# A decode block on one core: queries projected once per head in a loop, engines' code moved to new blocks, one store

## The chip, the core and the metric

The kernel runs on one core of a Trainium2 chip. The metric is the device time of one execution in microseconds; the core's engines are TensorE (PE, with its weight loads as PEld), VectorE (DVE), ScalarE (ACT), GpSimd (POOL) and SyncE (SP), and 16 DMA engines move data between HBM and SBUF.

## The reference

One decode step for two sequences (B = 2): pre-LayerNorm attention over a long cache, then a SwiGLU feed-forward, both with a residual. All data is float32.

```python
h  = x + A(_layernorm(x))            # x: [2, 1, 512]
h2 = h + B(_layernorm(h))

# A: 32 heads of 128, cache of 8192 keys and values per head and sequence
q = (x @ wq).reshape(B, 1, 32, 128).transpose(0, 2, 1, 3)      # wq: [512, 4096]
scores = einsum("bhqd,bhkd->bhqk", q, k_cache) * 128 ** -0.5   # [2, 32, 8192, 128]
o = einsum("bhqk,bhkd->bhqd", softmax(scores), v_cache)
A = o.transpose(0, 2, 1, 3).reshape(B, 1, 4096) @ wo           # wo: [4096, 512]

# B: F = 1792
B = (silu(x @ w_gate) * (x @ w_up)) @ w_down
```

The two caches are 268 MB each, wq and wo 8.4 MB each, the three feed-forward weights 3.7 MB each.

## The kernel before, in words

The program is written engine by engine: `do(engine, fn, sem)` appends an instruction to that engine's list, `wait(engine, point)` a wait for a semaphore's value, and `emit` writes the lists out. Nothing reorders them. All large loads stand in one list, `loads`, which SP issues in order on one DMA queue at the end of the function (L578 to L581); ahead of a load SP waits for `freed[...]`, the point at which the last reader of the slot is done.

There are three large SBUF slots of 64 KB in each partition: `kslot[0]`, `kslot[1]` and `vslot`. The loads are: wq into `vslot`; K0 (in two halves) and K1 into the key slots; then, in turn, V0, K2, V1, K3 and so on, V always into `vslot`, K into the key slot that its number names; at the end the last V, wo, w_gate, w_up and w_down. V0 waits for `freed["wq", 0]`, the last matmul that reads wq. V(i) waits for the matmuls of V(i-1), K(i) for VectorE's last reading of K(i-2).

A unit of work (32 in all, `U`) is two heads of one sequence. Half of the partitions (`HALF[0]`) hold the keys of one head, the other half those of the next. VectorE multiplies the keys by the query (L419) and sums over the 128 columns (L428), each in two parts. TensorE and ScalarE make the softmax (`pe_scores`, `softmax`), and TensorE multiplies by the values (`pe_values`, L329: 32 matmuls in four column groups of PSUM). TensorE's 31 first units are a hardware loop (`Fori`, L348); the last unit and the tail (wo, gate, up, down) are written out.

Ahead of the units comes the query projection. VectorE's multiply needs each query in all 64 partitions of its half. So the kernel before broadcasts each of the eight columns of the normalized and transposed x over 64 columns (`xT`, `xb`, L273 to L278) and uses these as weights: for each group of four head pairs and each sequence, eight matmuls (four chunks of 512 inputs, two halves) write a query into 64 equal rows of each half of a PSUM bank (L292, 64 matmuls). ScalarE copies each bank to `qsb` (L303). `q_done` holds these eight points, and `freed["wq", 0]` the last matmul.

The result is stored by two DMAs, one for each sequence, from SP and from ScalarE (L588). wo comes in three loads (`WO`: 20, 8 and 4 blocks), each waited for by the matmul that first reads it (L478).

Of the kernel before, what the change touches and what calls it, by code (L numbers as in the profile page):

```python
# [13 lines left out]
class Program:  # L14
# [16 lines left out]
    def wait(self, engine, *points):  # L31
        for s, value in points:
            if self.known[engine].get(s, 0) < value:
                self.known[engine][s] = value
                self.steps[engine].append(lambda e, s=s, v=value: e.wait_ge(s, v))  # L35
# [17 lines left out]
def decode_block(nc, x, k_cache, v_cache, wq, wo, w_gate, w_up, w_down, out):  # L53
    B, _, D = x.shape
    _, H, S, DH = k_cache.shape
    F = w_gate.shape[1]
    assert DH == P and B == 2 and D == 512 and F == 14 * P and H == 32 and S == 64 * P
    DC = D // P
# [4 lines left out]
    HP = P // 2  # L63
    NJ = S // HP
    U = B * H // 2
    MQ = H // 2
    HALF = (slice(0, HP), slice(HP, P))

# [8 lines left out]
    def sbuf(name, *shape, align=32):  # L77
        return nc.alloc_sbuf_tensor(name, list(shape), F32, align_bytes=align).ap()
# [25 lines left out]
    scores = [sbuf(f"s{n}", P, NJ) for n in range(2)]  # L104
# [4 lines left out]
    r = sbuf("r", P, 1)  # L109
# [9 lines left out]
    wide = [psum(f"wide{n}", P, D) for n in range(2)]  # L119
    bank = [psum(f"bank{n}", P, D) for n in range(4)]  # L120
# [16 lines left out]
    def alone(name):  # L137
        return g.sem(name)
# [3 lines left out]
    landed = {}  # L142
    freed = {}
    loads = []

    def k_src(cache, i):
        m, b = divmod(i, B)
# [70 lines left out]
    wait("scalar", ident_done)  # L218
    do("scalar", lambda e: e.dma_start(xs, x.rearrange("b s d -> (b s) d")), x_in := alone("x"), 16)
    p0 = do("gpsimd", lambda e: e.memset(sides, 0.0), s_pool)  # L220
    do("vector", lambda e: e.memset(nscale, -SCALE))
    half_done = do("vector", lambda e: e.memset(mhalf, -0.5), s_dve)
    wait("vector", ident_done)
# [46 lines left out]


    wait("vector", p)
    p = do("vector", lambda e: e.tensor_copy(xT, yt), s_dve)  # L273
    wait("vector", p)
    xb = osb.rearrange("p (c m) -> p c m", c=DC * B)
    xb_done = do(
        "vector",
        lambda e: e.tensor_copy(xb, xT.rearrange("p c b -> p (c b)")[:, :, None].to_broadcast([P, DC * B, HP])),  # L278
        s_dve,
    )  # L280
    wait("tensor", xb_done, landed[("wq", 0), 0])
    wqv = vslot.rearrange("p (c m k d) -> p c k m d", c=DC, k=2, d=DH)
    q_done = []
    for n, (m, b) in enumerate((m, b) for m in range(0, MQ, 4) for b in range(B)):
        ps = wide[n % 2].rearrange("p (j d) -> p j d", d=DH)
        if n > 1:
            wait("tensor", q_done[n - 2])
        for c in range(DC):
            for k in range(2):
                p = do(  # L290
                    "tensor",
                    lambda e, ps=ps, c=c, k=k, m=m, b=b: e.matmul(  # L292
                        ps[HALF[k]],
                        xb[:, c * B + b, :],
                        wqv[:, c, k, m : m + 4, :],
                        start=(c == 0),
                        stop=(c == DC - 1),
                    ),
                    s_pe if c == DC - 1 and k == 1 else None,
                )  # L300
        wait("scalar", p)
        q_done.append(
            do("scalar", lambda e, ps=ps, m=m, b=b: e.activation(qsb[:, b, m : m + 4, :], ps, AF.Copy), s_act)  # L303
        )
    freed["wq", 0] = p
    wait("tensor", consts_done)


# [1 line left out]
    base = g.count[s_pe]  # L310
# [34 lines left out]

    def pe_rounds(e):
        e.sem_inc(s_v, -16)
        with nc.Fori(0, U - 1, engines=[PE], head_slot={PE: 0}):  # L348
            pe_scores(e)
            e.wait_ge(s_v, 16)  # L350
            pe_values(e, vslot)
            pe_outputs(e)
            e.sem_inc(s_dve_pe, -2)
            e.sem_inc(s_act_pe, -2)
            e.sem_inc(s_v, -16)
        pe_scores(e)
        e.wait_ge(landed[("v", U - 1), 0][0], 16)
        pe_values(e, v_last)
        pe_outputs(e)
# [50 lines left out]
    for i in range(U):  # L410
        m, b = divmod(i, B)
        parts = 2
        n = NJ // parts
        wait("vector", q_done[m // 4 * B + b])
        for c in range(parts):
            wait("vector", landed[("k", i), c if i == 0 else 0])
            kt = k_view(i, c * n, n)
            qb = qsb[:, b, m, :][:, None, :].to_broadcast([P, n, DH])
            mult = do("vector", lambda e, kt=kt, qb=qb: e.tensor_tensor(kt, kt, qb, op=OP.mult), s_dve)  # L419
# [51 lines left out]
    for c in range(H):  # L471
# [3 lines left out]
        t = c % 4  # L475
# [21 lines left out]
    wait("scalar", normed)  # L497
    h1_done = do("scalar", lambda e: e.activation(h1, attn, AF.Copy), s_act)
# [28 lines left out]
    for t in range(4):  # L527
        do(
            "tensor",
            lambda e, t=t: e.matmul(  # L530
                f_ps[32 * t : 32 * t + 32, :], ident[:B, :32], h1[:, t * P : (t + 1) * P], start=True, stop=False
            ),
        )
    sg = rest[:, D : D + FQ]
# [43 lines left out]
    for item, e_, dst, src, sem in loads:  # L578
        if item in after:
            wait("sync", freed[after[item]])  # L580
        do("sync", lambda e, dst=dst, src=src: e.dma_start(dst, src), sem, 16)  # L581
    stored = []
    for b, engine in enumerate(("sync", "scalar")):
        wait(engine, res_done)
        stored.append(
            do(
                engine,
                lambda e, b=b: e.dma_start(out[b, 0, :].rearrange("(t m) -> t m", t=4), res[b::32, :]),  # L588
                alone(f"out{b}"),
                16,  # L590
            )
        )

    wait("sync", *stored)
# [42 lines left out]
```

## Time and profile before

| | |
|---|---|
| median of 3 runs | 1309.95 us (1309.79 to 1310.46) |
| the profiled execution | 1309.7 us |
| its span, first to last instruction | 1308.4 us |
| busy: PE, DVE, ACT | 434.1, 1131.3, 80.4 us |
| moved by DMA | 564.79 MB, 432 GB/s over the span |

In the rows, L329 is line 329 of the program before. A row of the timeline gives start, duration, engine, line, operation, output and inputs, and in brackets the engine's idle time ahead of it and what ended it. A row of DMA issues ends with the us from issue to landing. A float32 matmul leaves two records, and as many weight loads.

### The profile page before, as it was taken

Reading aid. Unit: us, or ns where it says so; the run is one execution under the profiler, and the core shown is the slowest. Engines: PE = TensorE matmul, PEld = TensorE weight load, DVE = VectorE, ACT = ScalarE, POOL = GpSimd, SP = SyncE. Lnnn points to the kernel's source line nnn. Section 1 sums busy time; section 2 is a strip of 40 time slices with the busy share of each in tenths; the row PEclk is TensorE's granted clock in tenths of the full one; section 3 lists DMA queues with packets and bytes.
Section 4 is the critical chain, followed back from the end, with each engine's and each line's share of the span. In section 5 each row is a group of like instructions: output and inputs, shape, how many; then the busy total and the mean of one; then the engine's idle time right before and its main releaser. Section 6 shows DMA issues by size and latency. Waiting matters only on the chain.

```text
span 1308.4 us, 6704 instructions
## 1 busy us (share of the span) xinstructions
PE 434.1 (33%) x2952; PEld 135.6 (10%) x2952; DVE 1131.3 (86%) x246; ACT 80.4 (6%) x271; POOL 2.9 (0%) x13
## 2 busy tenths in 40 slices
PE   3633223333223333311333321233332233332276
PEld 1210001011001011100101100001100010110022
DVE  1999988889888889988888988888998888898841
ACT  0100000000000000000000000000000000000010
POOL 0000000000000000000000000000000000000000
PEclk9865566666556666656666656666655666665578
DMA  9999999999999999999999999999999999999998
GB/s 403 440 437 439 427 447 423 443 423 445 421 445 425 441 435 431 443 427 443 423 445 421 445 425 441 433 433 443 427 441 425 441 425 441 429 439 435 431 423 371
DMA packets 11118, 564.79 MB, mean 432 GB/s; under 512 B 1242, under 2 KB 1250, under 8 KB 1636
## 3 DMA queue, kind: packets, MB, share of 16 engines
q1 hardware_dynamic: 11096, 564.67, 99.7%
q8 instruction: 5, 0.08, 0.0%
q14 instruction: 5, 0.04, 0.0%
q10 hardware_dynamic: 12, 0.01, 0.0%
HBM read 564.66 MB, written 0.00 MB: 432 GB/s over the span
## 4 chain that ended last, share of the span: by engine, by line
DMA 53%; DVE 45%; PE 1%; SPq 0%; issue 0%; DVEq 0%
DMA kslot<-in_A_k_cache_dram 48%; DVE kslot L419 22%; DVE s L428 22%; DMA kslot<-in_A_v_cache_dram 3%; DMA kslot<-in_B_w_down_dram 3%; PE opart L329 1%; DVE gm L372 0%; SPq L581 0%; DVE r L398 0%; PE bank L564 0%; DVE m L436 0%; DVE kslot L575 0%; DVEq L35 0%
## 5 line engine op out<-in xcount | busy, mean ns | idle before, releaser
L419 DVE TENSOR_TENSOR kslot<-kslot,qsb 128x8192 f32<-128x8192 f32 x64 | 555.6, 8681 | 119.5 <-DMA kslot<-in_A_k_cache_dram 119.5
L428 DVE TENSOR_REDUCE s<-kslot 128x64 f32<-128x8192 f32 x64 | 555.2, 8675 | 0.1
L329 PE MATMUL opart<-vslot,pz 128*8 128x512 f32 x1984 | 285.3, 740 | 246.5 <-DMA vslot<-in_A_v_cache_dram 246.5
L321 PE MATMUL bank<-gm,nscale 1*64 1x1 f32 x64 | 11.8, 250 | 358.4 <-DVE gm L372 358.4
L329 PEld LDWEIGHTS opart<-vslot,pz 128*8 128x8 f32 x1984 | 55.3, 104 | 450.4 <-DMA vslot<-in_A_v_cache_dram 249.1
L319 PE MATMUL bank<-ident,m 128*1 128x128 f32 x64 | 18.7, 395 | 168.1 <-DVE m L436 168.1
L321 PEld LDWEIGHTS bank<-gm,nscale 1*64 1x64 f32 x64 | 9.1, 199 | 374.4 <-DVE gm L372 374.4
L341 PE MATMUL bank<-rdiag,osb 128*128 128x2 f32 x256 | 33.7, 254 | 26.3 <-ACT osb L405 26.3
L400 ACT ACTIVATE rdiag<-fold,r 128x8 f32<-128x8 f32 x32 | 9.6, 301 | 484.6 <-DVE r L398 484.6
L379 ACT ACTIVATE nb<-bank 128x1 f32<-128x1 f32 x32 | 5.5, 171 | 551.6 <-PE bank L322 551.6
L341 PEld LDWEIGHTS bank<-rdiag,osb 128*128 128x128 f32 x256 | 31.0, 191 | 56.0 <-ACT osb L405 56.0
L292 PE MATMUL wide<-vslot,osb 128*64 128x512 f32 x128 | 29.9, 630 | 9.4 <-DMA vslot<-in_A_wq_dram 9.4
L324 PE MATMUL bank<-rs,sides 128*128 128x1 f32 x64 | 18.8, 363 | 41.5 <-ACT pz L385 41.5
L385 ACT ACTIVATE pz<-s,nb 64x128 f32<-64x128 f32 x64 | 25.5, 399 | 1.4
L405 ACT ACTIVATE osb<-opart 128x512 f32<-128x512 f32 x32 | 19.1, 597 | 72.4 <-PE opart L329 72.4
L324 PEld LDWEIGHTS bank<-rs,sides 128*128 128x128 f32 x64 | 16.1, 313 | 44.2 <-ACT pz L385 44.2
L319 PEld LDWEIGHTS bank<-ident,m 128*1 128x1 f32 x64 | 2.7, 81 | 171.6 <-DVE m L436 171.6
L292 PEld LDWEIGHTS wide<-vslot,osb 128*64 128x64 f32 x128 | 10.5, 146 | 28.0 <-issue 28.0
L385 ACT ACTIVATION_READ_ACCUMULATOR pz<-s,nb 64x1 f32 x64 | 11.8, 184 | 0.0
L322 PE MATMUL bank<-gm,nscale 1*64 1x1 f32 x64 | 11.8, 250 | 0.0
L235 DVE BATCH_NORM_STATS2 ln_stats<-attn 2x6 f32<-2x512 f32 x1 | 0.7, 686 | 11.4 <-PE attn L491 11.4
L451 DVE TENSOR_TENSOR om<-oT,quarter 128x256 f32<-128x256 f32 x1 | 0.4, 426 | 11.4 <-ACT oT L407 11.4
(60 smaller groups left out, 104.3 us busy)
## 6 DMA issues: line engine op xcount, KB each, us to landing
kslot<-in_A_k_cache_dram SPq DMA_DIRECT2D x2, 4096.0 KB, 35.8
vslot<-in_A_wo_dram SPq DMA_DIRECT2D x1, 5120.0 KB, 22.0
kslot<-in_B_w_gate_dram SPq DMA_DIRECT2D x1, 3584.0 KB, 31.7
kslot<-in_B_w_up_dram SPq DMA_DIRECT2D x2, 1792.0 KB, 37.5
vslot<-in_A_wo_dram SPq DMA_DIRECT2D x1, 2048.0 KB, 26.4
kslot<-in_B_w_down_dram SPq DMA_DIRECT2D x2, 1024.0 KB, 29.9
vslot<-in_A_wo_dram SPq DMA_DIRECT2D x1, 1024.0 KB, 28.4
kslot<-in_B_w_down_dram SPq DMA_DIRECT2D x1, 768.0 KB, 32.3
```

Of the source, the lines that this page charges most:

```text
L292: lambda e, ps=ps, c=c, k=k, m=m, b=b: e.matmul(ps[HALF[k]], xb[:, c * B + b, :], wqv[:, c, k, m : m + 4, :], start=(c == 0), stop=(c == D ...
L319: e.matmul(mrow, m1, ident, start=True, stop=True).then_inc(s_pe, 1)
L321: e.matmul(nb_ps[HALF[0]], nscale, gm[:, 0:1], start=True, stop=True)
L322: e.matmul(nb_ps[HALF[1]], nscale, gm[:, 1:2], start=True, stop=True).then_inc(s_pe, 1)
L324: e.matmul(den, sides.rearrange("p w a -> p (w a)"), rs, start=True, stop=True).then_inc(s_pe, 1)
L329: inst = e.matmul(opart[32 * t : 32 * t + 2 * W, :], pz[:, w, :], t_v[:, w * W * DH : (w + 1) * W * DH], start=(w < 4), stop=(w >= NW - 4),)
L341: inst = e.matmul(ot_ps, osb[:, a * DH : (a + 1) * DH], rdiag[:, a::W], start=(a == 0), stop=(a == W - 1))
L385: lambda e, k=k, h=h: e.activation(pz[h, :, k * W : (k + 1) * W], s[h].rearrange("p (w a) -> p w a", a=W), AF.Exp, bias=nb[h], scale=SCALE ...
L400: do("scalar", lambda e: e.activation(rdiag, diag, AF.Copy, scale=r))
L405: do("scalar", lambda e: e.activation(osb, opart, AF.Copy), s_act_pe)
L419: mult = do("vector", lambda e, kt=kt, qb=qb: e.tensor_tensor(kt, kt, qb, op=OP.mult), s_dve)
L428: lambda e, kt=kt, s=scores[i % 2][:, c * n : (c + 1) * n]: e.tensor_reduce(s, kt, axis=AX.X, op=OP.add),
```

## The change

**Queries.** The transposed x goes into `xq`, zero but for one column for each sequence and half, so that a matmul's weights are [128, 4]: eight matmuls (four chunks, two halves) leave the queries of four head pairs in four PSUM rows (half, sequence) of `wide[0]`. ScalarE copies these rows to `qrow`. Two more matmuls, one for each sequence, with a 0/1 matrix `pick` [4, 128] as weights, spread each query over the 64 rows of its half, into `q_ps`, and ScalarE copies both to `qsb`. This body runs four times (`NG`) in a hardware loop on TensorE. A semaphore `q` brings ScalarE's copies back to the loop. `freed["wq", 0]` is the eighth matmul of the last trip. VectorE's first unit waits for the first copy, all others for the last (`q_done` has two points).

**Code.** `next_block` puts the first instructions of TensorE, VectorE and ScalarE (there behind the load of x) at the start of the next block of instructions, by a branch over the padding. The loop of the units on TensorE begins at slot 80 of its block, before at slot 0.

**The rest.** x is loaded ahead of everything on ScalarE, without a wait for the identity matrix. GpSimd prepares `xq`, `pick` and `place`. The tail puts the two sequences at rows 0 and 16 of each group of 32 (`LANE`), before at 0 and 1, so that one DMA can store both. wo comes in two loads of 20 and 12 blocks.

```diff
+    LANE = 32 // B
+    place = sbuf("place", B, 32)
+    xq = sbuf("xq", P, DC, 2, 2 * B)
-    xT = sbuf("xT", P, DC, B)
+    qrow = osb[: 2 * B, :]
+    pick = om[: 2 * B].rearrange("p b (k r) n -> p b k (r n)", k=2)
+    s_q = g.sem("q")
...
+    BLOCK = {"tensor": 256, "vector": 128, "scalar": 128}
+    def next_block(engine):
+        do(engine, lambda e: e.addr_align(BLOCK[engine], offset=0, max_nops=0))
+    next_block("tensor")
+    next_block("vector")
...
-    WO = ((0, 20), (20, 8), (28, 4))
+    WO = ((0, 20), (20, 12))
...
+    do("scalar", lambda e: e.dma_start(xs, x.rearrange("b s d -> (b s) d")), x_in := alone("x"), 16)
+    next_block("scalar")
...
-    wait("scalar", ident_done)
-    do("scalar", lambda e: e.dma_start(xs, x.rearrange("b s d -> (b s) d")), x_in := alone("x"), 16)
+    xq_zero = do("gpsimd", lambda e: e.memset(xq, 0.0), s_pool)
...
-    wait("tensor", xb_done, landed[("wq", 0), 0])
+    lanes = xq.rearrange("p c k (l b) -> p c (k l) b", b=B)[:, :, ::3, :]
+    wait("vector", p, xq_zero)
+    xq_done = do("vector",
+        lambda e: e.tensor_copy(lanes, yt[:, :, None, :].to_broadcast([P, DC, 2, B])), s_dve)
+    wait("tensor", xq_done, pick_done, landed[("wq", 0), 0])
     wqv = vslot.rearrange("p (c m k d) -> p c k m d", c=DC, k=2, d=DH)
+    QM = 4
+    NG = MQ // QM
+    q_ps = [wide[1], bank[1]]
+    q_base = g.count[s_pe]
+    def pe_queries(e):
+        e.sem_inc(s_q, B)
+        with nc.Fori(0, NG, engines=[PE]) as n:
+            for j, (c, k) in enumerate((c, k) for c in range(DC) for k in range(2)):
+                inst = e.matmul(
+                    wide[0][: 2 * B, :].rearrange("p (j d) -> p j d", d=DH),
+                    xq[:, c, k, :],
+                    wqv[:, c, k, bass.ds(n * QM, QM), :],
+                    start=(j == 0), stop=(j == 2 * DC - 1))
+            inst.then_inc(s_pe, 1)
+            e.wait_ge(s_q, B + 1)
+            for b in range(B):
+                inst = e.matmul(q_ps[b], pick[:, b].rearrange("p k r -> p (k r)"), qrow,
+                                start=True, stop=True)
+            inst.then_inc(s_pe, 1)
+            e.sem_inc(s_q, -(B + 1))
-    for n, (m, b) in enumerate((m, b) for m in range(0, MQ, 4) for b in range(B)):
-        ps = wide[n % 2].rearrange("p (j d) -> p j d", d=DH)
-        if n > 1:
-            wait("tensor", q_done[n - 2])
...
+    for n in range(NG):
+        wait("scalar", (s_pe, q_base + 2 * n + 1))
+        do("scalar", lambda e: e.activation(qrow, wide[0][: 2 * B, :], AF.Copy), s_q)
+        wait("scalar", (s_pe, q_base + 2 * n + 2))
+        for b in range(B):
...
+    freed["wq", 0] = (s_pe, q_base + 2 * NG - 1)
...
-        with nc.Fori(0, U - 1, engines=[PE], head_slot={PE: 0}):
+        with nc.Fori(0, U - 1, engines=[PE], head_slot={PE: 80}):
...
-        wait("vector", q_done[m // 4 * B + b])
+        wait("vector", q_done[min(i, 1)])
...
-    hT_done = do("vector", lambda e: e.tensor_copy(hT[:, :, :B], yt), s_dve)
+    hT_done = do("vector", lambda e: e.tensor_copy(hT[:, :, ::LANE], yt), s_dve)
...
-    for b, engine in enumerate(("sync", "scalar")):
-        wait(engine, res_done)
...
+    wait("sync", res_done)
+    rows = out.rearrange("b s (t m) -> t (b s) m", t=4)
+    stored = do("sync", lambda e: e.dma_start(rows, res[::LANE, :]), alone("out"), 16)
+    wait("sync", stored)
```

TensorE's rows of the projection before: each names its line, output, inputs and what it waits for; `wide` is the PSUM bank, `vslot` holds wq, `osb` the broadcast x, and act is ScalarE's semaphore.

```order
L253 MATMUL bank<-ident,ln_y 128x2 x3
L292 MATMUL wide<-vslot,osb 64x512 [waits v,dve]
L292 MATMUL wide<-vslot,osb 64x512 x15
L292 MATMUL wide<-vslot,osb 64x512 [waits act]
L292 MATMUL wide<-vslot,osb 64x512 x7
...
L348 ISA [waits pool]
L348 UNCONDITIONAL_BRANCH
```

After, the same place holds the loop's body once (here `osb` is `qrow`, `om` is `pick`, ISA a step on registers, and q the semaphore of ScalarE's copies; two of the eight query matmuls are shown):

```order
L332 UNCONDITIONAL_BRANCH [waits v,dve,pool]
L332 ISA
L334 MATMUL wide<-vslot,xq 4x512
L334 ISA
L334 MATMUL wide<-vslot,xq 4x512
...
L344 MATMUL wide<-osb,om 128x512 [waits q]
L344 MATMUL bank<-osb,om 128x512
L332 REGISTER_ALU
L332 COMPARE_AND_BRANCH
```

The half-width matmuls (64 rows of output) are gone, the wait for ScalarE moved from every second group's start into the middle of each trip, and the wait for wq (v) stands ahead of the loop. ScalarE's rows at the same place, before:

```order
L303 ACT_TABLE_LOAD
L303 ACTIVATE qsb<-wide 128x512 [waits pe] x8
L379 ACTIVATE nb<-bank 128x1 [waits pe]
L385 ACTIVATE pz,rs<-s,nb 64x32x4 [waits pool,act]
L385 ACTIVATE pz,rs<-s,nb 64x32x4
```

and after:

```order
L354 ACT_TABLE_LOAD
L354 ACTIVATE osb<-wide 4x512 [waits pe]
L360 ACTIVATE qsb<-wide 128x512 [waits pe]
L360 ACTIVATE qsb<-bank 128x512 [waits act]
L354 ACTIVATE osb<-wide 4x512 [waits pe]
L360 ACTIVATE qsb<-wide 128x512 [waits pe]
L360 ACTIVATE qsb<-bank 128x512
```

Eight copies became twelve, three for each trip: the four rows, then one bank for each sequence.

More of the change, by code (lines that the diff above doesn't have):

```diff
@@ L217, in decode_block @@
     )
-    wait("scalar", ident_done)
-    do("scalar", lambda e: e.dma_start(xs, x.rearrange("b s d -> (b s) d")), x_in := alone("x"), 16)
+    xq_zero = do("gpsimd", lambda e: e.memset(xq, 0.0), s_pool)
+    p0 = do("gpsimd", lambda e: e.memset(pick, 0.0), s_pool)
+    wait("gpsimd", p0)
+    pick_done = do(
+        "gpsimd",
+        lambda e: e.affine_select(
+            out=pick,
+            in_=pick,
+            compare_op=OP.not_equal,
+            fill=1.0,
+            base=0,
+            pattern=[[-1, B], [-B, 2], [0, HP]],
+            channel_multiplier=1,
+        ),
+        s_pool,
+    )
     p0 = do("gpsimd", lambda e: e.memset(sides, 0.0), s_pool)
+    p1 = do("gpsimd", lambda e: e.memset(place, 0.0), s_pool)
     do("vector", lambda e: e.memset(nscale, -SCALE))
@@ L268, in decode_block @@
         p0 = do("gpsimd", lambda e, t=t, value=value: e.memset(t, value), s_pool)
-    consts_done = p0
[L272 to L276, printed above, removed]
+    wait("gpsimd", p1)
+    p0 = do(
+        "gpsimd",
+        lambda e: e.affine_select(
+            out=place,
+            in_=place,
+            compare_op=OP.not_equal,
+            fill=1.0,
+            base=0,
+            pattern=[[-1, 32]],
+            channel_multiplier=LANE,
+        ),
+        s_pool,
+    )
@@ L282, in decode_block @@
     wqv = vslot.rearrange("p (c m k d) -> p c k m d", c=DC, k=2, d=DH)
-    q_done = []
-    for n, (m, b) in enumerate((m, b) for m in range(0, MQ, 4) for b in range(B)):
-        ps = wide[n % 2].rearrange("p (j d) -> p j d", d=DH)
-        if n > 1:
-            wait("tensor", q_done[n - 2])
[L288 to L304, printed above, removed]
@@ L305, in decode_block @@
-    freed["wq", 0] = p
+    QM = 4
[10 more added lines that the diff above has]
+                    wqv[:, c, k, bass.ds(n * QM, QM), :],
+                    start=(j == 0),
+                    stop=(j == 2 * DC - 1),
+                )
+            inst.then_inc(s_pe, 1)
+            e.wait_ge(s_q, B + 1)
+            for b in range(B):
+                inst = e.matmul(
+                    q_ps[b], pick[:, b].rearrange("p k r -> p (k r)"), qrow, start=True, stop=True
+                )
+            inst.then_inc(s_pe, 1)
+            e.sem_inc(s_q, -(B + 1))
@@ new lines, in decode_block @@
+    g.steps["tensor"].append(pe_queries)
+    q_done = []
+    for n in range(NG):
[3 more added lines that the diff above has]
+        for b in range(B):
+            told = (n, b) in ((0, 0), (NG - 1, B - 1))
+            c = do(
+                "scalar",
+                lambda e, n=n, b=b: e.activation(
+                    qsb[:, b, n * QM : (n + 1) * QM, :], q_ps[b].rearrange("p (j d) -> p j d", d=DH), AF.Copy
+                ),
+                s_act if told else s_q,
+            )
+            if told:
+                wait("scalar", c)
+                do("scalar", lambda e: e.sem_inc(s_q, 1))
+                q_done.append(c)
@@ L306, in decode_block @@
+    freed["wq", 0] = (s_pe, q_base + 2 * NG - 1)
+    g.count[s_pe] = q_base + 2 * NG
     wait("tensor", consts_done)
@@ L530, in decode_block @@
             lambda e, t=t: e.matmul(
-                f_ps[32 * t : 32 * t + 32, :], ident[:B, :32], h1[:, t * P : (t + 1) * P], start=True, stop=False
+                f_ps[32 * t : 32 * t + 32, :], place, h1[:, t * P : (t + 1) * P], start=True, stop=False
             ),
@@ L581, in decode_block @@
         do("sync", lambda e, dst=dst, src=src: e.dma_start(dst, src), sem, 16)
-    stored = []
-    for b, engine in enumerate(("sync", "scalar")):
-        wait(engine, res_done)
[L585 to L594, printed above, removed]
+    wait("sync", res_done)
+    rows = out.rearrange("b s (t m) -> t (b s) m", t=4)
+    stored = do("sync", lambda e: e.dma_start(rows, res[::LANE, :]), alone("out"), 16)
+    wait("sync", stored)
     ids = sorted(s.num for s in g.sems)
```

3 lines of the change are left out of this document (2 added, 1 removed).

## The prediction

> **What bounds the kernel now.** I read the DMA part of the page first, then the chain, the timeline of the first 130 us, the DMA view by stretches, and the timeline of the tail. The page, then the chain:
>
> ```profile
> q1 hardware_dynamic: 11096, 564.67, 99.7%
> DMA 53%; DVE 45%; PE 1%; SPq 0%; issue 0%; DVEq 0%
> ```
>
> Queue q1, which carries every large load, is busy for 99.7% of the span on all 16 DMA engines. The chain calls 45% DVE because it follows K0 to K2 through VectorE, but VectorE then waits for keys again. So the time is: when the stream starts, 564.67 MB at its steady rate, stretches in which the queue is empty or an engine of it lags, and what comes after the last byte. No saving on a compute engine counts unless it moves one of these. The timeline, by start, duration and engine:
>
> ```profile
> 0.73 0.40 SPq L581 DMA_DIRECT2D vslot<-in_A_wq_dram  x1
> 22.80 29.86 PE L292 MATMUL wide<-vslot,osb 128*64 128x512 f32 x128 [9.44 <-DMA vslot<-in_A_wq_dram]
> 32.44 8.69 DVE L419 TENSOR_TENSOR kslot<-kslot,qsb 128x8192 f32<-128x8192 f32 x1 [18.42 <-DMA kslot<-in_A_k_cache_dram]
> 52.69 0.33 SPq L581 DMA_DIRECT2D vslot<-in_A_v_cache_dram  x1
> 67.21 0.33 SPq L581 DMA_DIRECT2D kslot<-in_A_k_cache_dram  x1
> 82.09 8.59 PE L329 MATMUL opart<-vslot,pz 128*8 128x512 f32 x64 [3.49 <-DMA vslot<-in_A_v_cache_dram]
> 120.70 9.76 PE L329 MATMUL opart<-vslot,pz 128*8 128x512 f32 x64 [7.08 <-DMA vslot<-in_A_v_cache_dram]
> ...
> vslot<-in_A_wq_dram SPq DMA_DIRECT2D x1, 21.9
> ```
>
> V0 and V1 are used as they land, 38.61 us apart with one K load between: 19.3 us for 8.39 MB. wq landed at about 22.7, and K0, K1 and V0 are three such loads, so V0 was due at 80.6. It came at 82.1: the last of its engines lost about 1.45 us on the way. The DMA view of three stretches (0 to 100, 100 to 1250, 1250 to the end) shows what else ran:
>
> ```profile
> q8 instruction: 2, 0.03, 0.1%
> ...
> q14 instruction: 4, 0.03, 0.0%
> ...
> q8 instruction: 3, 0.05, 0.3%
> ```
>
> Two packets of code of 16 KB lie in the first stretch, none in the long loop of TensorE, three in its straight tail: queue q8 is TensorE's code. I read the 1.45 us as the price of one such packet in a full queue, on the engine that fetched it. A lag like that stays to the end, since nothing lets the engine catch up.
>
> The slot that matters is vslot: V0 may only be issued when the projection has read wq, at 52.69. K0 and K1 fill the queue until about 22.7 + 38.6 = 61.3, so V0 has 8.6 us in hand. That cover is what the change spends.
>
> **The projection, part by part.** The rows of TensorE's order above show it: 64 matmuls, whose waits on act are for a PSUM bank two groups back and are free, became 32 plus 8 that spread, and each of the four trips now stops in its middle for ScalarE (wait on q). How long is one matmul? Weight loads of line 292 by start, then a lone 512-column matmul of the tail:
>
> ```profile
> 28.01 0.16 PEld L292 LDWEIGHTS wide<-vslot,osb 128*64 128x64 f32 x2 [0.27 <-issue]
> 28.44 0.16 PEld L292 LDWEIGHTS wide<-vslot,osb 128*64 128x64 f32 x2 [0.27 <-issue]
> ...
> L487 PE MATMUL attn<-xs,ident x2: 586/586/587, 1282.2 to 1282.6; 2*2 2x512 f32 x2
> L292 PE MATMUL wide<-vslot,osb x128: 592/592/1116, 22.8 to 52.1; 128*64 128x512 f32 x128
> ```
>
> A matmul has two records. In line 292 one matmul starts every 0.43 us, although each record lasts 0.592: the two halves run side by side. In line 487, without a partner, the two records start 0.4 apart, so one matmul takes 0.85. The new query matmuls all write the same four PSUM rows, and have no partner. So 32 at 0.85 take what 64 at 0.43 took: the 29.86 us stand, the slow first 4 us included. The spreads are extra: two of 0.85, 1.71 per trip, and three trips lie ahead of the last group's reading of wq: 5.1 us. The hop to ScalarE and back:
>
> ```profile
> 1250.53 0.60 ACT L405 ACTIVATE osb<-opart 128x512 f32<-128x512 f32 x1 [2.27 <-PE opart L329]
> 1251.18 0.97 PEld L341 LDWEIGHTS bank<-rdiag,osb 128*128 128x128 f32 x8 [1.66 <-ACT osb L405]
> ...
> L498 ACT ACTIVATE kslot<-attn 2x512 f32<-2x512 f32 x1 | 0.6, 587 | 3.8 <-DVE ln_y L245 3.8
> ```
>
> 0.60 of copy (0.59 even for two rows), 0.08 for both signals, 0.16 in which the last matmul drains (0.592 less 0.43), and some 0.1 for a 128-column weight load (0.97 for eight): 0.94, three times 2.8. V0's issue: 52.69 + 5.1 + 2.8 = 60.6. To this come two unknowns. The loop's branch and register steps: below nothing is excluded, since they are added; above, no row shows one alone, and ScalarE's 0.60 copy and the spreads cover them; I take 0.2, bounds 0 and 2. And the code fetch that beginning in the next block starts at 0.8 us, as wq starts to flow: if it meets wq's stream it costs its engine up to the 1.45 us above and wq lands that much later; if it goes out before the first data it costs nothing. I take 0.7. V0 is issued at 61.5, bounds 60.6 and 64.
>
> By then the queue is empty. A load of this size into an empty queue is the wq row: 21.9 us from issue to landing, 2.6 more than the 19.3 it takes in line. V0 lands at 61.5 + 21.9 = 83.4 instead of 82.05: **+1.35 us**, bounds -0.2 (60.6, and 21.3: the 19.3 with the 2.0 that the 2 KB store of the tail below takes from issue to end) and +3.9. [...] I go by the row, which is this queue's.
>
> VectorE starts K0 later: the first query is ready at 22.8 + 9.0 (eight matmuls, 4.4 us of them slow, as before) + 0.94 + 1.71 + 0.65 = 35.1, not at 32.44, so K2 goes out at 69.9 instead of 67.21, when V0 has until 83 to run. That is covered, and would be uncovered only if K0 ended some 12 us later still; then the queue would run dry again. The later key loads keep 34.9 us of VectorE against 38.6 of DMA.
>
> **Code fetches.** Before, the first two packets lag two engines by 1.45 us, and the three late ones fall on engines that have this much to spare. After, the empty queue lets all 16 engines start V0 level, so the early lag vanishes into the gap; but TensorE's tail of 172 matmuls is unchanged and is still fetched in a full queue, and now each fetch is paid: **+1.2**, bounds 0 (they hit leaders, or come when the data has ended) and +1.9 (the same engine also takes one 8 KB packet of another engine's code). [...]
>
> **The tail.**
>
> ```profile
> 1279.11 0.10 PEld L478 LDWEIGHTS wide<-vslot,oq 128*2 128x2 f32 x4 [0.33 <-issue]
> 1288.40 5.75 PE L512 MATMUL wide<-kslot,hT 128*32 128x448 f32 x32 [0.97 <-DMA kslot<-in_B_w_gate_dram]
> ...
> vslot<-in_A_wo_dram SPq DMA_DIRECT2D x1, 1024.0 KB, 28.4
> 1250.53 1.28 SPq L581 DMA_DIRECT2D vslot<-in_A_wo_dram  x3
> 1306.28 0.65 SPq L588 DMA_DIRECT2D out_dram<-kslot  x1
> 1306.29 0.61 ACTq L588 DMA_DIRECT2D out_dram<-kslot  x1
> ...
> SPq L35 <- DMA out_dram<-kslot: 1.3, 1, 1.3
> ```
>
> The second wo load now ends where the third did, 1251.4 + 28.4 = 1279.8, and its first block is wanted at 1279.1: TensorE waits 0.7 us more. The gate projection after it waited 0.97 us for its own weights, which hide it. One store instead of two, issued at once on two queues, saves what the second holds SP: I take -0.1, bounds 0 and -0.3. SP issues wo in two steps instead of three, ahead of loads that wait for VectorE: nothing. The constants on GpSimd and the x load moved ahead are done before wq lands.
>
> **Rivals.**
> 1. *The gap swallows the lag and nothing brings it back* (this ends not slower). V0 lands in step with before if it is issued by 82.05 - 21.9 = 60.15, and the late fetches hit leaders or cost nothing. With V0 issued at 60.6, 21.3 to land and no late lag: -0.2 + 0 - 0.2 = -0.4 us, 1309.3 in this execution, 1309.6 as a median. [...] With one of these three failing it gives +0.3 to +1.5. For it: the sum of known rows is 60.6. Against: every unknown adds. It decides where V0 is issued before about 61 us.
> 2. *The loop is dearer than its matmuls.* A branch or register step that TensorE's queue doesn't hide, of 1 us a trip, or a clock that falls in the 0.94 us stops, adds 3 us or more: 1315.6 upward. It decides from about 1 us a trip. If the clock never rose for matmuls of four columns, the 32 would take their 27 us twice: about 1340. Against the clock: it rose for two-column matmuls in the tail, and it fell only 5 us after the projection's end at 52.7 (column PEclk, third from the right):
>
> ```profile
> 57.00:58.00 1.00, 0.00 (x0) 0.00 (x0) 1.00 (x1) 0.00 (x0) 0.00 (x0) 0.97 0.45 197
> 58.00:59.00 1.00, 0.00 (x0) 0.00 (x0) 0.97 (x2) 0.00 (x0) 0.00 (x0) 0.50 1.96 852
> 1277.00:1279.00 2.00, 2.00 (x24) 0.44 (x20) 0.00 (x0) 0.00 (x0) 0.00 (x0) 1.00 1.13 483
> ```
>
> 3. *The change does not cost TensorE time*: four-column matmuls at 0.43. Then V0 is issued at 60.6 - 13.7 = 47, in time; the two early fetches are gone and with them 1.45, and the store saves 0.1: 1308.4. Line 487 speaks against it.
>
> **How the numbers follow.** 1.35 + 1.2 - 0.1 = +2.45 us on the profiled execution's 1309.7 (1.3 above its span), which stands 0.25 below the median of the runs, 1309.95. So 1312.4; since the unknowns of the loop can only add, I put it at 1312.6. A difference of 0.2%, 2.6 us, is about what a measurement of this kernel can tell from no change, and the forecast stands on that bound: its own range is 1311 to 1315. Chances: forecast 0.62, of which 0.43 above the bound; rival 1 0.25; rival 2 0.09; rival 3 0.04, counted as faster though its price lies inside the bound. Slower 0.52, same 0.44, faster 0.04. For 8 in 10 the range goes from 1310.2, which leaves out the low end of rival 1 and rival 3 (0.12), to 1316.0, which leaves out most of rival 2 (0.06).
>
> **What would show it.** Right: V0's issue in the queue at 60.5 to 63 with DMA share falling for one or two us just before its data; 0.85 us between query matmuls; ScalarE's copies between; VectorE's first multiply at 35; V0 used at 82.5 to 85, and 38.6 us from V0 to V1 as before. The chain should still end in w_down's loads and the new store. Wrong: V0 issued before 59, an unbroken DMA share there, wq landing at 22.7 with all later loads in step, or a last w_down load earlier than 1305.

## The result, and the profile after

The changed kernel takes 1315.25 us (median of six runs, 1314.42 to 1317.8) against 1309.74 (six runs, 1309.62 to 1310.46): a ratio of 1.0045, 95% interval 1.0034 to 1.0056. The forecast was 1312.6 with a range of 1310.2 to 1316.0: the sign is right, the range holds the median, the forecast's own range (1311 to 1315) does not. The runs are further apart than before's, 3.4 us against 0.8, and they fall into two groups: four at 1314.4 to 1315.4, two at 1317.6 and 1317.8. The profiled execution is one of the upper two: 1317.55, span 1315.9.

From the page, queues and the first line of the chain:

```profile
q1 hardware_dynamic: 10956, 564.67, 99.2%
q8 instruction: 4, 0.07, 0.0%
q14 instruction: 6, 0.05, 0.0%
DMA 53%; DVE 45%; PE 2%; issue 0%; ACT 0%; SPq 0%
```

The stream of the large loads is still the bound, but q1 has fallen from 99.7% to 99.2% of a longer span. The timeline of the first 130 us (start, duration, engine; in brackets the idle time before and what ended it) shows where it was empty:

```profile
23.93 9.88 PE L334 MATMUL wide<-vslot,xq 128*4 x16 [18.47 <-DMA vslot<-in_A_wq_dram]
33.85 0.59 ACT L354 ACTIVATE osb<-wide 4x512 f32<-4x512 f32 x1 [30.82 <-PE wide L334]
34.49 1.12 PE L344 MATMUL wide<-osb,om 4*128 4x512 f32 x2 [0.68 <-ACT osb L354]
36.40 8.73 PE L334 MATMUL wide<-vslot,xq 128*4 x16
37.13 8.69 DVE L484 TENSOR_TENSOR kslot<-kslot,qsb 128x8192 f32<-128x8192 f32 x1 [31.46 <-ACT qsb L360]
47.71 7.03 PE L334 MATMUL wide<-vslot,xq 128*4 x16
57.58 8.43 PE L334 MATMUL wide<-vslot,xq 128*4 x16
66.03 0.33 SPq L646 DMA_DIRECT2D vslot<-in_A_v_cache_dram  x1
71.89 0.33 SPq L646 DMA_DIRECT2D kslot<-in_A_k_cache_dram  x1
87.90 8.64 PE L394 MATMUL opart<-vslot,pz 128*8 128x512 f32 x64 [4.62 <-DMA vslot<-in_A_v_cache_dram]
126.52 4.45 PE L394 MATMUL opart<-vslot,pz 128*8 128x512 f32 x20 [8.14 <-DMA vslot<-in_A_v_cache_dram]
```

V0 is issued at 66.03 instead of 52.69, used 21.87 later at 87.90 instead of 82.09, and V1 38.62 after V0, as before. The four groups of query matmuls do the same work and take 9.88, 8.73, 7.03 and 8.43 us. The view by stretches says why. Its columns are the length of the stretch, the busy times of TensorE, its weight loads, VectorE, ScalarE and GpSimd, the granted clock (the share of its full clock that TensorE was given), the DMA share and GB/s:

```profile
36.00:40.00 4.00, 4.00 (x7) 0.61 (x6) 2.87 (x1) 1.19 (x2) 0.00 (x0) 0.57 0.99 426
40.00:48.00 8.00, 7.32 (x17) 1.62 (x16) 7.97 (x2) 0.77 (x2) 0.00 (x0) 1.00 1.03 446
57.00:61.00 4.00, 4.00 (x6) 0.57 (x6) 4.00 (x1) 1.09 (x2) 0.00 (x0) 0.57 0.61 262
61.00:66.00 5.00, 5.00 (x12) 0.87 (x10) 4.97 (x2) 0.00 (x0) 0.00 (x0) 1.00 0.00 0
```

In before's projection the clock was full after the first 4.4 us. Here it fell to half near the start of the second and of the fourth trip (0.57 is the mean of a stretch at two levels): 6 to 7 records of matmuls in 4 us, not 11. The first group begins at half clock too: its records start 0.85 us apart until 29.8 us and 0.43 from there. The clock column doesn't show that, since it reads 1.00 ahead of a trace's first clock record, here at 29.70. And from 61 to 66 the DMA share is 0.00: K1's data is through (its last part is signalled at 61.95) and V0 is not yet issued. The tail:

```profile
1287.49 2.76 PE L543 MATMUL wide<-vslot,oq 128*2 128x512 f32 x24 [2.39 <-DMA vslot<-in_A_wo_dram]
1296.03 4.89 PE L577 MATMUL wide<-kslot,hT 128*32 128x448 f32 x32 [0.63 <-DMA kslot<-in_B_w_gate_dram]
1304.44 1.71 PE L577 MATMUL wide<-kslot,hT 128*32 128x448 f32 x16 [1.53 <-DMA kslot<-in_B_w_up_dram]
1314.01 0.69 SPq L649 DMA_DIRECT2D out_dram<-kslot  x1
```

TensorE waits 2.39 us for wo's second load, and after it still for gate, up and w_down. The end stays with w_down's last load.

The profiled execution's +7.85 us, by the landings of each load's sixteen parts in the trace: V0's last part at 87.86 instead of 82.05, +5.81; w_down's last part 1225.17 later instead of 1223.38, +1.79; from there to the span's end 2.9 instead of 3.0, -0.1; around the span 1.65 instead of 1.3, +0.35.

### The profile page after: what moved, and what is told of

It reads as the page before. It is cut to its first block, busy times and chain, and to the rows that moved or that the text cites. A ratio compares the mean times of both kernels' runs of the same rounds, so it can differ in the third digit from the quotient of the medians.

```text
span 1315.9 us, 6660 instructions
## 1 busy us (share of the span) xinstructions
PE 443.0 (34%) x2904; PEld 134.0 (10%) x2904; DVE 1130.8 (86%) x245; ACT 82.5 (6%) x275; POOL 3.8 (0%) x18
## 3 DMA queue, kind: packets, MB, share of 16 engines
q1 hardware_dynamic: 10956, 564.67, 99.2%
## 4 chain that ended last, share of the span: by engine, by line
DMA 53%; DVE 45%; PE 2%; issue 0%; ACT 0%; SPq 0%
DMA kslot<-in_A_k_cache_dram 45%; DVE kslot L484 22%; DVE s L493 22%; DMA kslot<-in_A_v_cache_dram 3%; DMA kslot<-in_B_w_down_dram 3%; DMA vslot<-in_A_wq_dram 2%; PE wide L334 1%; PE opart L394 1%; DVE gm L437 0%; PE bank L629 0%; DVE r L463 0%; PE wide L344 0%; PE bank L344 0%; SPq L646 0%; ACT qsb L360 0%
## 5 line engine op out<-in xcount | busy, mean ns | idle before, releaser
L334 PE MATMUL wide<-vslot,xq 128*4 x64 | 34.1, 694 | 18.5 <-DMA vslot<-in_A_wq_dram 18.5
L334 PEld LDWEIGHTS wide<-vslot,xq 128*4 128x4 f32 x64 | 5.8, 96 | 45.6 <-issue 45.6
L501 DVE TENSOR_REDUCE m<-s 128x1 f32<-128x128 f32 x32 | 9.2, 286 | 1.1
## 6 DMA issues: line engine op xcount, KB each, us to landing
vslot<-in_A_wo_dram SPq DMA_DIRECT2D x1, 5120.0 KB, 23.2
```

Of the source, the lines that this page charges most:

```text
L334: inst = e.matmul(wide[0][: 2 * B, :].rearrange("p (j d) -> p j d", d=DH), xq[:, c, k, :], wqv[:, c, k, bass.ds(n * QM, QM), :], start=(j ...
```

## Experiments

**What a late V0 costs by itself.** The kernel before got matmuls on constants between the projection and the signal that frees wq's slot: 16, 10 and 6 of them (late_v0, late_10, late_6).

```
+    LATE = 16                                     # 10, 6
+    def pe_late(e):
+        with nc.Fori(0, LATE, engines=[PE]):
+            e.matmul(bank[2][:HP, :], ident[:, :HP], osb, start=True, stop=True).then_inc(s_pe, 1)
+    g.steps["tensor"].append(pe_late)
+    g.count[s_pe] += LATE
-    freed["wq", 0] = p
+    freed["wq", 0] = (s_pe, g.count[s_pe])
```

> The kernel before, with 16 matmuls of 512 columns on constants (0.85 us each by the rows of after, 13.6 us together) behind the projection, ahead of the signal that frees wq's slot; nothing else moves. Theory L: V0 issued at 66 to 67, used 21.9 later at 88 to 89, so the time rises by 5.5 to 8: 1315.2 to 1317.7, like after. If a late V0 is not the price (theories C and T): 1309.7 to 1311. If the empty queue also lets all engines restart level and nothing brings the early lag back, 1.4 less than the first figure.

> The kernel late_v0 with 10 matmuls instead of 16, so that V0 is issued at 61.0 to 61.3, just ahead of K1's last data and where the prediction had put it (61.5). Theory P (a load issued into an emptying queue takes its 21.2 to the first engine's and 21.8 to the last engine's landing, so it costs from an issue at 58.9 on): V0 lands at 82.3 on the first engine and 83.0 on the last, the time is 2 to 2.6 above before, 1311.8 to 1312.5. Theory Q (as long as the issue is ahead of the queue's end nothing is lost): 1309.7 to 1310.3.

> The kernel late_v0 with 6 matmuls instead of 16: V0 issued at 57.7 to 57.9, some 5 us later than before. By theory P this lies inside the cover (58.9): V0 lands at 80.1 to 80.3 on the first engine, time 1309.6 to 1310.4. If every microsecond of a later issue costs, 1313 or more.

V0's issue and first use in late_v0, then late_10, then late_6:

```profile
66.19 0.33 SPq L589 DMA_DIRECT2D vslot<-in_A_v_cache_dram  x1
88.00 7.58 PE L337 MATMUL opart<-vslot,pz 128*8 128x512 f32 x52 [9.51 <-DMA vslot<-in_A_v_cache_dram]
```

```profile
60.69 0.33 SPq L589 DMA_DIRECT2D vslot<-in_A_v_cache_dram  x1
82.54 9.55 PE L337 MATMUL opart<-vslot,pz 128*8 128x512 f32 x64 [4.10 <-DMA vslot<-in_A_v_cache_dram]
```

```profile
57.92 0.33 SPq L589 DMA_DIRECT2D vslot<-in_A_v_cache_dram  x1
82.14 8.70 PE L337 MATMUL opart<-vslot,pz 128*8 128x512 f32 x64 [3.65 <-DMA vslot<-in_A_v_cache_dram]
```

late_v0 takes 1317.32 (ratio 1.0057, 1.0044 to 1.0071), late_10 1312.30 (1.0019, 1.0010 to 1.0028), late_6 1310.08 (1.0002, 0.9993 to 1.0011). A late V0, with nothing else changed, costs +7.5, +2.4 and +0.2. late_v0 has its V0 where the profiled execution of after had it, and its time too. With 21.81 and 21.85 us from issue to first use the price of a load into the drained queue holds. late_6 shows the cover: V0 issued 5.2 us later than in before, still used at 82.1. In the landings the first of the 16 DMA engines has V0 at 80.1 in before, at 82.0 in late_10 (82.5 on the last; with its issue, too, 0.3 to 0.6 earlier than I expected) and at 87.4 in late_v0, 21.2 to 21.3 after the issue in the last two. So the cover, the time by which V0's issue can slip for nothing, ends at 80.1 - 21.2 = 58.9, and from there a microsecond of V0's issue costs about one of the time: +2.4 with the issue at 60.69, +7.5 at 66.19.

**Which part of the change.** q_alone is the kernel before with the new query loop only; rest_alone is the kernel after with the old projection.

```
# q_alone: before, plus xq, pick, pe_queries and ScalarE's two copies; not next_block, head_slot, WO, store
# rest_alone: after, with
+    for n, (m, b) in enumerate((m, b) for m in range(0, MQ, 4) for b in range(B)):
+        ...
+                        ps[HALF[k]], xb[:, c * B + b, :], wqv[:, c, k, m : m + 4, :],
-    g.steps["tensor"].append(pe_queries)
```

> The kernel before with the new query loop alone; blocks, loop head, store and wo as before. Theory L (V0 is issued late because the loop holds wq too long): V0 issued at 64 to 66 us instead of 52.7, used at 86 to 88 instead of 82.1, and the time is 4 to 7 us above before: 1314 to 1317. Theory C (the code's new block starts and the fetches they make are what costs): without them V0's lateness matters little, 1309.5 to 1311.5. Theory T (the tail: wo in two loads, the store): 1309.5 to 1310.

> The kernel after with the projection of before (64 matmuls in two column halves, four waits per group free), all else as after. Theory L: V0 issued at 53 to 54, no empty queue, used at 82 to 83; the time is that of before within 1 us either way, 1309.0 to 1310.7. Theory C or T: most of the 5.5 us stay, 1313 to 1316.

Timeline of q_alone (V0's issue and first use), its DMA view of 62 to 87 us, then the timeline of rest_alone:

```profile
62.10 0.33 SPq L621 DMA_DIRECT2D vslot<-in_A_v_cache_dram  x1
85.45 9.70 PE L369 MATMUL opart<-vslot,pz 128*8 128x512 f32 x64 [4.39 <-DMA vslot<-in_A_v_cache_dram]
```

```profile
q8 instruction: 1, 0.02, 0.2%
...
vslot<-in_A_v_cache_dram SPq DMA_DIRECT2D x1, 23.3
```

```profile
52.61 0.33 SPq L606 DMA_DIRECT2D vslot<-in_A_v_cache_dram  x1
81.99 9.87 PE L354 MATMUL opart<-vslot,pz 128*8 128x512 f32 x64 [2.63 <-DMA vslot<-in_A_v_cache_dram]
```

q_alone takes 1314.11 (1.0041, 1.0028 to 1.0055), rest_alone 1310.51 (1.0005, 0.9996 to 1.0014). The query loop makes the loss; of the rest no effect over the measurement's uncertainty is seen. q_alone's V0 went out ahead of the 64 to 66 I expected; its trace has one fall of the clock in the loop, after's two. In q_alone a packet of TensorE's code fell into V0's own stream, and V0 took 23.3 us to land instead of the 21.8 that the same view gives in after: 1.5 us more, the price that the prediction had put on such a packet. no_blocks (below) has such a packet in V0's stream as well, and V0 lands 23.2 after its issue.

**The clock.** filled is the kernel after with four matmuls of 128 columns on constants in each stop; after_again is the kernel after once more.

```
             inst.then_inc(s_pe, 1)
+            for _ in range(4):
+                e.matmul(bank[2][: 2 * B, :P], xq[:, 0, 0, :], ident, start=True, stop=True)
             e.wait_ge(s_q, B + 1)
```

> The kernel after with four matmuls of 128 columns on constants (0.21 us each, 0.85 together) put into each stop, between a trip's query matmuls and the wait for ScalarE; they delay the spread by 0.2 to 0.5 us a trip. Theory S (the stops let the granted clock fall, and two falls cost 1.9 and 1.6 us of the profiled loop): the clock stays at 1.00 from the first query to the last, all later trips take 9.9 to 10.4, V0 is issued at 63 to 64.5 instead of 66.0, time 1314.0 to 1315.3, and the runs lie within 1 us of each other instead of 3.4. Theory N (few columns of weights, so a narrow array, let it fall): falls as in after, V0 at 65 to 68, 1315 to 1318, the same spread of runs.

> The kernel after once more, to have a second profiled execution of it. Its runs fell in two groups, 1314.4 to 1315.4 and 1317.6 to 1317.8. If the number of clock falls in the query loop makes the groups: a profiled execution of the lower group shows one fall or none and V0 issued at 62.5 to 64.5, one of the upper two falls and V0 at about 66. If something later in the program makes them: V0's issue is 66 in either group, or the lower group shows two falls.

The query groups and V0's issue in filled, two of its stretches, then the later groups, V0's issue and a stretch of after_again:

```profile
23.92 8.81 PE L334 MATMUL wide<-vslot,xq 128*4 x16 [18.45 <-DMA vslot<-in_A_wq_dram]
...
54.93 7.03 PE L334 MATMUL wide<-vslot,xq 128*4 x16
61.99 0.33 SPq L648 DMA_DIRECT2D vslot<-in_A_v_cache_dram  x1
```

```profile
36.00:40.00 4.00, 4.00 (x11) 0.78 (x9) 3.82 (x1) 0.74 (x2) 0.00 (x0) 1.00 1.00 434
57.00:61.00 4.00, 4.00 (x11) 0.84 (x10) 4.00 (x1) 0.00 (x0) 0.00 (x0) 1.00 0.61 262
```

```profile
36.37 8.53 PE L334 MATMUL wide<-vslot,xq 128*4 x16
...
57.10 7.03 PE L334 MATMUL wide<-vslot,xq 128*4 x16
64.16 0.33 SPq L646 DMA_DIRECT2D vslot<-in_A_v_cache_dram  x1
```

```profile
36.00:40.00 4.00, 4.00 (x6) 0.57 (x6) 2.89 (x1) 1.20 (x2) 0.00 (x0) 0.57 0.99 426
```

With the stops filled the clock, once risen in the first group, stays at 1.00 through the loop, each later group takes 7.03, and the nine runs lie within 1.3 us: 1313.65 (1.0028, 1.0019 to 1.0038). Theory S had the clock right; V0 and the time come out below its ranges. V0 is issued 4 us earlier than in after: some 3.1 are the two falls, and 1.1 is a first group of 8.81 instead of 9.88 us. By its median filled is 1.6 us under after, with four matmuls more per trip, since they run while TensorE would have stood; the two intervals still touch. after_again (1315.75; 1.0052, 1.0038 to 1.0065) was caught with one fall instead of two: V0 at 64.16, 1315.32 us, the lower group. Its five runs again make two groups, 1314.5 to 1315.8 and 1317.6 to 1318.7. That the number of falls makes the groups fits these two executions, and q_alone, no_blocks and wo_three have runs in two groups as well, where filled has one; but the other runs have no trace to show it.

Which stops go with a fall can be counted in the traces. In all fourteen of them the granted clock changes only at points that are whole multiples of 3.41 us apart, and a fall in the query loop lasts one such step. Six steps of after follow, with the time in them that query matmuls alone were busy (the columns are the length, TensorE, its weight loads, the granted clock, the DMA share and GB/s):

```profile
33.11:36.53 3.42, 0.83 (x3) 0.09 (x2) 1.00 0.95 412
36.53:39.94 3.41, 3.41 (x5) 0.52 (x4) 0.50 0.93 404
43.35:46.77 3.42, 1.77 (x5) 0.17 (x2) 1.00 1.33 575
46.77:50.18 3.41, 2.47 (x6) 0.53 (x7) 1.00 0.80 346
53.59:57.01 3.42, 1.15 (x3) 0.09 (x1) 1.00 0.93 402
57.01:60.42 3.41, 2.84 (x4) 0.48 (x5) 0.50 0.71 308
```

Steps with 0.83 and 1.15 us of query matmuls are followed by a step at half clock, the one with 1.77 is not. The pause of 0.68 lies in all three. What differs is how much of the spread matmuls, which read only four partitions (`4*128` in their rows), lies in the step with it. I counted for every step at full clock, in all traces up to 1300 us, the time without a matmul that reads 128 partitions and streams 32 columns or more; the other matmuls of these programs read four partitions at most, or stream two columns at most. Of 479 falls, 478 come at the end of a step with 2.03 us or more of such time; the 831 steps that end without a fall have 2.04 or less. Within the query phase the two are further apart: 2.19 and more with a fall, 2.01 and less without. So in this count the spreads go with the pauses. Behind filled's last trip the clock fell with 0.35 us of pause in the step and 1.9 of spreads, while 1.86 us of pure pause in a step behind before's projection did not bring it down. A trip has 2.6 us of pause and spreads together. Where the steps lie against the program differs between executions (the first rise comes 2.8 to 5.8 us after the first query matmul), and with it the number of falls. In filled 1.84 us are left in each trip, less than the 2.03 from which falls were counted, wherever the steps lie. This is a reading of the traces; no run changes the partitions of the spreads alone.

V0's issue against the time of the same execution, less the median of before beside it; the rule is late_10's +2.4 at 60.7 and one for one above it:

| execution | V0 issued | difference | by the rule |
|---|---|---|---|
| filled | 61.99 | +3.5 | +3.7 |
| q_alone | 62.10 | +3.9 | +3.8 |
| no_blocks (below) | 62.26 | +3.1 | +4.0 |
| wo_three (below) | 63.64 | +4.8 | +5.3 |
| after_again | 64.16 | +5.5 | +5.9 |
| after | 66.03 | +7.8 | +7.7 |
| late_v0 | 66.19 | +7.5 | +7.9 |

The rule fits six of the seven to 0.5 us or better; no_blocks lies 0.9 under it.

**The start blocks and wo.** no_blocks is after without the three calls of `next_block`, wo_three is after with `WO = ((0, 20), (20, 8), (28, 4))`.

> The kernel after without the three starts in a new block; the code runs on from where it stands. Theory L: wq lands on its last engine at 22.6 instead of 23.4 and the first query matmul starts at 23.1 to 23.2 instead of 23.9, so V0 is issued about 0.8 earlier than in after at the same number of clock falls, and the time is 0.5 to 1 lower, 1313.6 to 1314.8 as a median; a fetch may fall into V0's own stream, but at the end the spread of the engines stays 1.65 to 1.9 whatever the fetches do. If the blocks saved what a fetch in the loop costs: 1315 to 1317.

> The kernel after with wo in three loads again. The chain at the end runs through w_down's last load, which is set by the stream: the wait of 2.39 us for wo's second load shrinks to under 1.5 and moves to the waits for gate, with no gain: within 1 us of after, 1314.3 to 1316. If wo's second load costs on the path, 1.5 to 2.4 less, 1312.8 to 1313.8.

Query matmuls and V0's issue in no_blocks, then TensorE's waits for wo and for up in wo_three:

```profile
23.15 8.54 PE L331 MATMUL wide<-vslot,xq 128*4 x16 [17.69 <-DMA vslot<-in_A_wq_dram]
62.26 0.33 SPq L643 DMA_DIRECT2D vslot<-in_A_v_cache_dram  x1
```

```profile
1279.05 9.66 PE L543 MATMUL wide<-vslot,oq 128*2 128x512 f32 x64 [0.32 <-ACT oq L534]
1301.96 1.71 PE L577 MATMUL wide<-kslot,hT 128*32 128x448 f32 x16 [0.94 <-DMA kslot<-in_B_w_up_dram]
```

wo_three takes 1315.31 (1.0049, 1.0035 to 1.0063), as after does: the wait of 2.39 us is gone and nothing is gained, so wo's two loads cost nothing. no_blocks has wq 0.8 us earlier as expected, but its median of 1316.52 (1.0047, 1.0034 to 1.0061; after's interval lies within 0.0005 of it) is not the 1313.6 to 1314.8 I expected: two runs at 1313.1 and 1313.6, three at 1316.5 to 1317.6. The lower two are about 1 us below after's lower group; why the upper group came more often in these five stays open. In the spans there is one more trace of the blocks: time less span is 1.62 to 1.82 in the runs of each kernel with both the blocks and the new query code (after, filled, wo_three, tiled), 1.27 to 1.51 in all others, no_blocks, q_alone and rest_alone among them. Some 0.35 us of the loss lies outside the span; I did not find out why it takes both.

**The lag of the engines.** short_tail is late_v0 with most of TensorE's tail left out (4 of wo's 32 matmuls, 4 of 16 each for gate and up, 4 of w_down's 56 are done).

> The kernel late_v0 with most of TensorE's tail left out (4 of wo's 32 matmuls, 4 of 16 each for gate and up, 4 of w_down's 56 are done; all loads and waits stay), so that its code is some 27 KB shorter. In late_v0 the engines were 0.6 us apart at V0 and 1.87 at the end. Theory F (TensorE's code fetched late into a full queue makes the end spread): the end spread falls to 0.6 to 1.2 and the time by 0.6 to 1.2, to 1316.1 to 1316.8. If the spread grows by itself over the stream: 1.8 still, 1317.0 to 1317.5.

The code packets of late_v0 from 1240 us on, then those of short_tail:

```profile
q8 instruction: 3, 0.05, 0.2%
```

```profile
q8 instruction: 1, 0.02, 0.1%
```

Theory F fell: with one late packet of TensorE's code instead of three the engines still end 1.74 us apart, and the time is 1317.83 (1.0061, 1.0048 to 1.0075). By the landings the lag is back before any of those packets: 0.6 and 0.5 us between first and last engine at V0, 1.89 and 1.71 at 1150 us, with only four 8 KB packets in between, of queue q14, which the shorter tail leaves as it was (four from 100 to 1240 us in both runs, one after) and which I take for other engines' code. The lag grows at the packets and hardly moves between them: in late_v0 from 0.5 to 1.2 us at the first two (215 and 237 us), and from 1.2 to 2.0 at the fourth (963 us). In after two 8 KB packets before 600 us took it from 0.4 to 1.2, a third at 1148 us to 1.3, and the 16 KB one at 1264 us to 1.9. In every trace the end is 1.6 to 2.0.

**Query matmuls side by side.** tiled is after with the query matmuls of the four slices of D written to PSUM rows 0, 32, 64 and 96, so that they can run side by side. ScalarE copies 128 rows instead of four, the spread matmuls read all 128 partitions and sum the four groups, and the trips are written out. tiled_plain has besides the loop head of before, no start blocks and wo in three loads.

```
-                    wide[0][: 2 * B, :].rearrange("p (j d) -> p j d", d=DH),
+                    opart[32 * c : 32 * c + 2 * B, :].rearrange("p (j d) -> p j d", d=DH),
...
-                    start=(j == 0), stop=(j == 2 * DC - 1),
+                    start=(k == 0), stop=(k == 1),
```

> [...] Theory L: a trip takes 8 x 0.21 + 0.94 + 1.71, about 4.4 us warm and 6 to 8 the first; V0 issued at 38 to 46, no empty queue, 1309 to 1311. If four-row matmuls in separate row groups do not overlap (0.85 each), V0 is issued at 64 to 66 and the time stays 1314 to 1317. Theory C or T: 1313 to 1316 in either case.

> A version that might beat both: queries in four row groups as in the tiled run, one store, and from the kernel before the loop head, no new blocks and wo in three loads. V0 issued at 42 to 43, no empty queue. The stream then sets the time as in before; one store instead of two saves 0.2: 1309.3 to 1310.2. If the end spread of the engines falls with TensorE's smaller code, down to 1308.5.

Timeline of tiled: the last of its four query groups, V0's issue and first use:

```profile
41.39 1.90 PE L335 MATMUL opart<-vslot,xq 128*4 128x512 f32 x16
43.35 0.33 SPq L647 DMA_DIRECT2D vslot<-in_A_v_cache_dram  x1
82.09 9.74 PE L395 MATMUL opart<-vslot,pz 128*8 128x512 f32 x64 [2.70 <-DMA vslot<-in_A_v_cache_dram]
```

A group takes 1.90 us instead of 7.03, V0 goes out 9 us earlier than in before, and tiled takes 1310.20 (1.0002, 0.9993 to 1.0011), tiled_plain 1309.94 (0.9999, 0.9990 to 1.0008). That undoes the loss; it beats before by nothing that these runs can tell, for a V0 that is earlier than 58.9 only waits in the queue (issued at 43.35 here and at 57.92 in late_6, used at 82.1 in both). tiled's clock doesn't fall between its groups once it has risen (32.95 us, in the second trip): its spreads read 128 partitions, so in the count above only the pauses of some 0.7 us are left.

## Why the prediction was right in sign and short in size

**The bound, and V0 as the step that carries the change: right.** late_v0 reproduces the profiled execution with V0's lateness alone. Term by term, on the profiled execution, V0 cost +5.81 (forecast +1.35), the lag +1.79 (+1.2), the store -0.1 (-0.1), and +0.35 lies outside the span, where the sum had nothing. That the range to 1316.0 holds the median is in part luck: V0's issue fell outside its own bounds of 60.6 to 64, and two of the six runs lie above the range.

**21.9 us into the drained queue: right.** 21.87 in after. With V0 at 60.69, near the forecast's 61.5, late_10 costs +2.4, the forecast's +2.45. The agreement of the sum is luck in part: V0's last part lands only 0.45 later there (82.50), where the forecast had 1.35, and 2.2 us come behind it, where it had 1.2.

**V0's issue at 61.5: wrong, 66.03.** It has three parts. The query groups were to take the old 29.86; they took 9.88 + 8.73 + 7.03 + 8.45 = 34.1, +4.2. Of this, 3.1 are the two falls: the assumption that failed is the clock that the prediction took to hold through the 0.94 us stops. It weighed the stop alone; in the count above the 1.9 us of spreads behind it go with the pause of 0.68. The other 1.1 is the first group's longer start at half clock. In filled, where the clock holds and rises sooner, the groups take 8.81 + 3 x 7.03 = 29.9. Stops, spreads and loop together were put at 8.15; the three gaps between groups took 8.0. The first query matmul came at 23.93 instead of 22.80, where 0.7 had been allowed: +0.4 (after's first 16 KB packet of TensorE's code starts at 1.92 us, in wq's stream; before's at 43.84). So 61.5 + 4.2 + 0.4 - 0.15 = 66.0. Rival 2 named this clock, with 1315.6 upward, and got 0.09, on the evidence that the clock fell only 5 us after the old projection's end. That row spoke of one pure pause, not of short ones with four-partition matmuls behind them.

**Rival 1, decided "before about 61": wrong point.** late_10 was issued at 60.69 and lost 2.4. The 82.05 it started from was the lagging engine's landing; the first engine has V0 at 80.1, so the cover ends at 58.9.

**The late code fetches, +1.2: 0.6 short, though inside its bounds, and the cause right only in part.** The lag did come back after the level restart: from 0.59 to 1.77 between first and last engine, 1.79 on the last. But short_tail shows that TensorE's tail is not needed for it; 8 KB packets of q14, which the sum had only in its upper bound, bring it back too. With one packet of TensorE's code in its own stream, q_alone's V0 took 23.3 us to land, 1.5 more than in after.

**wo's wait of 0.7, hidden: hidden, but 2.39.** wo_three shows that it costs nothing. **The store, -0.1:** as sized. **VectorE's first multiply at 35.1:** 37.13, with a first group that began 1.1 us later and took 0.9 longer than put; K2 went out at 71.89, covered as said. **Outside the span:** 0.35 us that the sum did not have, its cause open.

## What to carry to other kernels

When a change spends the cover of a load, size that cover from the engine that lands first and count the load's own start-up as part of it (21.2 us from issue to the first engine's landing, against 19.3 for such a load in line): here 52.7 to 58.9, not to the queue's end at 61.3. When it cuts a run of matmuls into bursts with a hand-off in each, price the loop at full and at half clock, look at what the matmuls behind the stop read (here 0.68 us of pause with 1.9 us of matmuls over four partitions went with two falls of the clock in four trips), and look whether other work can run in it. Ask of a matmul with few output rows whether it has a partner in other row groups before you price it: 0.85 us each alone here, 1.90 for eight in four row groups.

## What the runs showed of the hardware that I had not expected

Behind pauses of 0.68 us, with 1.9 us of matmuls over four partitions after them, the granted clock fell to half for 3.41 us, in two trips of after and in one of after_again. In the fourteen traces, up to 1300 us, 478 of 479 falls come at the end of a 3.41 us step that has 2.03 us or more without matmuls over 128 partitions and 32 columns or more; in that count the matmuls over four partitions stand with the pauses. Matmuls of four output rows, 0.85 us alone, run four at a time in row groups 32 apart: eight in 1.90. And with the queue full the landings of the engines moved apart at packets of 8 KB of code, and the lag stayed: in late_v0 the first and the last engine were 0.6 us apart at V0 and 1.9 at 1150 us, with four such packets in between.
